# Moving one weight load of a linear-attention and feed-forward kernel from the head of the load queue to a later place

## The chip, the cores and the metric

The kernel runs on one core of a Trainium2 chip. A core has five engines with instruction streams of their own: TensorE (PE, matrix products; its weight loads are listed apart as PEld), VectorE (DVE), ScalarE (ACT), GpSimd (POOL) and SyncE (SP), which here mostly issues transfers. Transfers between the chip's main memory and the on-chip memory, and within the latter, run on 16 DMA engines. The metric is the device time of one execution in microseconds; the median of several executions counts.

## The reference

Two blocks follow each other. The first is a gated linear recurrence for each of 4 batches and 8 heads, over 768 steps with head size 48:

```python
f = 1.0 / (1.0 + np.exp(-f_logit))
for t in range(S):
    state = f[:, :, t, :, None] * state + np.einsum('bhd,bhe->bhde', k[:, :, t], v[:, :, t])
    y[:, :, t] = np.einsum('bhd,bhde->bhe', q[:, :, t], state)
```

The second takes y, with the heads side by side, as x (3072 tokens of 384 values) and computes `(x @ w_a * (x @ w_b)) @ w_out`, with w_a and w_b of 384 x 1536 and w_out of 1536 x 384. The weights arrive as 64-bit floats, everything else as 32-bit floats.

## The kernel before

**Units.** The recurrence is cut into units. A unit is one batch, one half of the sequence (384 steps) and four heads; units 0 and 1 are the two groups of four heads of the first half of batch 0, units 2 and 3 the second half, and so on, 16 in all. For a unit the kernel computes running products of f and of their inverses (`front_parts`: sigmoids on ScalarE, an affine step on GpSimd, scans L333 and L346 on VectorE), multiplies k and q with them (L350), and then has only matrix products and a mask: `scores` (L396), `mask` (L409, VectorE), `turn` and `turned` (k transposed: L421 on PE, copied on ScalarE L430), `gains` (L445), `carried` (sums of states, L474, VectorE), `within` (L504, needs the mask), `across` (L530). `out_of_bank` (L553) copies the result out of PSUM, and `stores_of` (L575) writes it by transfers into `xT`, the input of the feed-forward block; these are the y transfers. Those of units 0 and 1 are issued by SP, by GpSimd and (unit 1) by ScalarE.

**Weights.** `weight_pieces` cuts the weights into pieces in the order of use: pieces 0 and 1 are the first 128 columns of w_b and w_a (384 KB each as 64-bit words), pieces 2 and 3 the next 256 columns of w_b and of w_a (768 KB each), and so on. `load_weights` (L269) issues the load of the next piece on SP into one of four places of `raws4`, or, for pieces 4 and 5, into `groups`. `from_double` makes 32-bit floats of a piece: on ScalarE Abs (L71), Identity (L72) and, later, Sign (L75); on GpSimd a clamp (L73) behind the Abs; on VectorE a shift (L78) and an addition into `w_ba` (L83). `begin(n)` emits the first and second part up to piece n-1, `end(n)` the VectorE part, and `end` also issues the next load from piece 6 on. So piece 3 is read by `begin(4)` and finished by `end(4)`.

**Order.** Each engine carries out its instructions in the order in which they are written. The first part of the program is written out by hand (L1030 to about L1145), until unit 3 is done; `up(0, i)` (L619) are the first products of the feed-forward block, each of six matrix products with columns 128 i to 128 i + 127 of w_b and w_a, and `product` multiplies the two results (copy L640 on ScalarE, L645 on VectorE). After that the remaining units and the feed-forward block are interleaved by a planner that works from stated durations; it comes after all that the change touches.

Around the change the loads stand in this order on SP's queue: f of units 0 and 1; for each of these k, q, a weight piece, v; f of unit 2; pieces 2 and 3; k and q of unit 2. Then SP has nothing to issue until the y transfers of units 0 and 1. After these come f of unit 3 (which waits until GpSimd has filled its buffer, L231), piece 4, v of unit 2, piece 5, k and q of unit 3, piece 6, v of unit 3, piece 7, f of unit 4.

The part of the program behind the change, in the order written: `begin(3)`, `end(2)`, the inverse scans of unit 2, the loads just named, `up(0, 0)`, k and q of unit 2 multiplied, `begin(4)`, sigmoids of unit 3, `end(3)`, `end(4)`, `turn(2)`, `scores(2)`, `up(0, 1)`, `mask(2)`, `product`, `hand_on`, `turned(2)`, `begin(5)`, `within(2)`, `gains(2)`, `up(0, 2)`, `end(5)`, and so on. `up(0, 1)` is the first that needs pieces 2 and 3. The calls `keep_up` (L1020) put matrix products without use between others.

Of the kernel before, what the change touches and what calls it, by code (L numbers as in the profile page):

```python
# [109 lines left out]
def kernel(  # L110
# [29 lines left out]
    with ExitStack() as pools:  # L140
        again, ending = by_quotients(pools, tc, q, k, f_logit, v, moe_w_a, moe_w_b, moe_w_out, out, ident, weights, bad, banks)
# [12 lines left out]
def by_quotients(ctx, tc, q, k, f_logit, v, moe_w_a, moe_w_b, moe_w_out, out, ident, weights, bad, ps_f):  # L154
# [61 lines left out]
    def load_unit(u, names="fkqv"):  # L216
        for do in loads_of(u, names):
            do()

    def loads_of(u, names="fkqv"):  # L220
        if u >= NU:
            return
        b, half, qd = unit(u)
        t = sets[u % NSET]
        cols = slice(half * BLK, half * BLK + BLK)

        def load(to, src):
            nc.sync.dma_start(out=to, in_=src)

        if u - NSET in FIRST and "f" in names:  # L230
            nc.gpsimd.memset(t["f"], 30.0)  # L231
        for nm, src in (("f", f_logit), ("k", k), ("q", q)):
            if nm not in names:
                continue
            if nm == "f" and u in FIRST:

                for par in range(2):
                    row = ((b * H + 4 * qd + par) * D) * S + half * BLK
                    rows = bass.AP(src.tensor, src.offset + row, [[S, R], [2 * D * S, 2], [1, BLK]])
                    yield partial(load, t[nm][R * par:R * par + R], rows)  # L240
                continue
            heads = src[b].rearrange("(n two) d s -> two d n s", two=2)
            for par in range(2):
                yield partial(load, t[nm][R * par:R * par + D], heads[par][:, 2 * qd:2 * qd + 2, cols])
        if "v" in names:
            yield partial(
                load,
                t["v"].rearrange("s n c x -> s n (c x)"),
                v[b, 2 * qd:2 * qd + 2, :, half * NC:half * NC + NC].rearrange("n s c two d -> s n (c two d)"),
            )  # L250
# [5 lines left out]
    def load_weights(n=1):  # L256
        for _ in range(n):
            if len(raws) == len(todo):
                return
            dst, src, (k, m) = todo[len(raws)]  # L260
            raw = dst
            if src.dtype != FP32:

                if len(raws) in EARLY:
                    raw = groups[:, EARLY.index(len(raws))].bitcast(mybir.dt.uint64)
                else:
                    raw = next(raw_places)
                raw = raw[:, 0:k * m].rearrange("p (k m) -> p k m", k=k)
            nc.sync.dma_start(out=raw, in_=src)  # L269
            raws.append(raw)  # L270
# [728 lines left out]
    with tc.manual_schedule():  # L999
# [38 lines left out]
            load_weights()  # L1038
            load_unit(u, "v")
        load_unit(2, "f")  # L1040
        load_weights(2)
        load_unit(2, "k")
        load_unit(2, "q")
        for part in parts[0][1:]:
# [39 lines left out]
        emit_all(parts[2][2])  # L1084


        load_unit(3, "f")
        load_weights()
        load_unit(2, "v")
# [598 lines left out]
```

## Time and profile before

| What | Value |
|---|---|
| Median of 3 runs | 589.61 us (589.22 to 590.11) |
| Profiled execution, time | 590.78 us |
| Profiled execution, span from first to last instruction | 588.9 us |
| PE busy | 568.4 us, 97% of the span |
| VectorE busy | 412.0 us, 70% |
| ScalarE busy | 257.5 us, 44% |
| GpSimd busy | 90.4 us, 15% |
| Mean granted TensorE clock | 0.996 |
| Moved by DMA | 49.42 MB, mean 84 GB/s |
| Loads of w_a in pieces of 768 KB | 4, median 11.8 us from issue to landing |

The profile is of one execution. Times in it count from the start of the span. "L71" is line 71 of the kernel; a line can be that of a helper. A row of the timeline gives start, length (from the first to the last of the instructions merged), engine, line, operation, output and inputs with their sizes, and in brackets how long the engine had been idle and what ended that. SPq stands for transfers issued by SP. A row of the chain gives start, length and what the end of the program waited for in that stretch; "issue" is time in which the engine waited for nothing that the profile shows. DMA share is the mean busy share of the 16 engines; values a little over 1 occur because packets overlap.

### The profile page before, as it was taken

To read this page: it belongs to the slowest core of one execution; us is meant where nothing else is said; L and a number is where in the kernel's file an instruction comes from. 1 tells how busy PE (TensorE), PEld (TensorE's weight loads), DVE (VectorE), ACT (ScalarE), POOL (GpSimd) and SP (SyncE) were. 2 spreads that over 40 slices of the span, in tenths; PEclk is the share of its full clock that TensorE was granted. 3 is DMA by queue.
4 is the path that set the end of the run, shared out by engine and by line. 5 is a ranking of instruction groups with operands and counts; after the bars stand their busy time and mean duration, and the time that the engine had idled before them with its cause. 6 is when DMAs were issued, how large, how long until landed. Compare 5 with 4: busy or idle time off the path is not lost.

```text
span 588.9 us, 13930 instructions
## 1 busy us (share of the span) xinstructions
PE 568.4 (97%) x5796; PEld 510.7 (87%) x5796; DVE 412.0 (70%) x782; ACT 257.5 (44%) x494; POOL 90.4 (15%) x73
## 2 busy tenths in 40 slices
PE   2789999999999999999999999999999999999997
PEld 1546655558999999999999999999999999999997
DVE  6799644599878869876997777837785165836651
ACT  5587668652122554246520444326431345235400
POOL 7365456454000000000000000000000000000000
PEclk9999999999999999999999999999999999999999
DMA  8789489089444123034105400041001100000001
GB/s 198 200 237 303 133 241 297 20 151 186 102 133 107 52 53 102 1 90 100 43 2 129 119 11 2 2 113 36 3 1 48 48 2 0 2 28 0 1 29 32
DMA packets 33576, 49.42 MB, mean 84 GB/s; under 512 B 3984, under 2 KB 25280, under 8 KB 33504
## 3 DMA queue, kind: packets, MB, share of 16 engines
q1 hardware_dynamic: 30000, 42.19, 26.2%
q0 software_dynamic: 3088, 5.92, 5.9%
q8 instruction: 47, 0.77, 0.6%
q10 hardware_dynamic: 416, 0.34, 0.2%
q14 instruction: 25, 0.20, 0.1%
HBM read 33.23 MB, written 4.72 MB: 64 GB/s over the span
## 4 chain that ended last, share of the span: by engine, by line
PE 91%; DVE 5%; issue 2%; ACT 1%; DMA 1%; SPq 0%; DVEq 0%; ACTq 0%
PE ps_f L745 39%; PE ps_f L847 28%; PE ps_f L619 15%; PE ps_y L504 2%; PE ps_y L530 2%; PE ps_x L445 1%; PE ps_x L396 1%; PE ps_x L421 1%; DVE inv L346 1%; DVE q_in L350 1%; DVE groups L333 1%; DMA f_in<-in_f_logit_dram 1%; DVE at L409 0%; DVE groups L737 0%; DVE spare L346 0%
## 5 line engine op out<-in xcount | busy, mean ns | idle before, releaser
L619 PE MATMUL ps_f<-xT,w_ba 128*128 128x384 f32 x288 | 95.8, 490 | 0.7 <-DVE w_ba L83 0.6
L1335 ACT COPY sums<-ps_f 128x384 f32<-128x384 f32 x120 | 57.6, 480 | 76.2 <-PE ps_f L745 68.5
L619 PEld LDWEIGHTS ps_f<-xT,w_ba 128*128 128x128 f32 x288 | 53.7, 190 | 37.8 <-ACT spare L75 1.2
L1335 ACT COPY groups<-ps_f 128x384 f32<-128x384 f32 x120 | 57.6, 481 | 61.3 <-PE ps_f L745 40.7
L745 PE MATMUL ps_f<-xT,w_ba 128*128 128x192 f32 x384 | 78.5, 327 | 0.0
L745 PEld LDWEIGHTS ps_f<-xT,w_ba 128*128 128x128 f32 x384 | 64.7, 190 | 0.3
L73 POOL TENSOR_SCALAR sums<-sums 128x768 f32<-128x768 f32 (+1 forms) x20 | 52.6, 2629 | 34.5 <-ACT sums L71 34.4
L745 PE MATMUL ps_f<-groups,w_ba 128*128 128x192 f32 x288 | 54.9, 326 | 0.0
L745 PE MATMUL ps_f<-x_sums,raw 128*128 128x192 f32 x288 | 53.7, 330 | 0.5 <-DVE groups L737 0.5
L329 POOL TENSOR_SCALAR inv<-inv 128x768 f32<-128x768 f32 x14 | 13.6, 972 | 261.2 <-ACT inv L326 217.0
L847 PE MATMUL ps_f<-w_out,sums 128*128 128x192 f32 x288 | 51.9, 327 | 0.0
L847 PE MATMUL ps_f<-w_out,groups 128*128 128x192 f32 x288 | 51.8, 329 | 0.0
L847 PE MATMUL ps_f<-spare,sums 128*128 128x192 f32 x288 | 49.5, 327 | 0.0
L745 PEld LDWEIGHTS ps_f<-x_sums,raw 128*128 128x128 f32 x288 | 47.0, 190 | 2.6 <-ACT sums L1335 1.0
L745 PEld LDWEIGHTS ps_f<-groups,w_ba 128*128 128x128 f32 x288 | 48.0, 190 | 0.1
L847 PEld LDWEIGHTS ps_f<-w_out,groups 128*128 128x128 f32 x288 | 47.2, 190 | 0.7
L847 PEld LDWEIGHTS ps_f<-w_out,sums 128*128 128x128 f32 x288 | 47.3, 190 | 0.2
L847 PEld LDWEIGHTS ps_f<-spare,sums 128*128 128x128 f32 x288 | 47.0, 190 | 0.1
L737 DVE TENSOR_TENSOR sums<-ps_f,sums 128x384 f32<-128x384 f32 x60 | 32.7, 553 | 16.9 <-PE ps_f L745 12.9
L737 DVE TENSOR_TENSOR sums<-sums,groups 128x768 f32<-128x768 f32 x36 | 34.3, 953 | 11.8 <-ACT groups L1335 11.2
L745 PE MATMUL ps_f<-xT,raw 128*128 128x192 f32 x192 | 39.4, 328 | 0.2 <-ACT groups L1335 0.2
L745 PE MATMUL ps_f<-x_sums,w_ba 128*128 128x192 f32 x192 | 39.3, 327 | 0.0
(150 smaller groups left out, 850.7 us busy)
## 6 DMA issues: line engine op xcount, KB each, us to landing
raw<-w_ba POOLq DMA_DIRECT2D x11, 512.0 KB, 8.3
k_in<-in_k_dram SPq DMA_DIRECT2D x32, 144.0 KB, 4.4
q_in<-in_q_dram SPq DMA_DIRECT2D x32, 144.0 KB, 4.5
v_in<-in_v_dram SPq DMA_DIRECT2D x16, 288.0 KB, 5.1
raw<-in_moe_w_out_dram SPq DMA_DIRECT2D x6, 768.0 KB, 4.8
out_dram<-o SPq DMA_DIRECT2D x22, 192.0 KB, 1.9
f_in<-in_f_logit_dram SPq DMA_DIRECT2D x28, 144.0 KB, 3.0
xT<-y SPq DMA_DIRECT2D x44, 72.0 KB, 2.1
```

The lines of the kernel that those rows point to most:

```text
L73: nc.gpsimd.tensor_scalar(h, h, HI_MIN, HI_MAX, ALU.max, ALU.min)
L329: nc.gpsimd.tensor_scalar(inv, inv, EXP_K, 1.0, ALU.mult, ALU.add)
L333: nc.vector.tensor_tensor_scan(F[:, c], F[:, c], none, math.exp(MIDDLE), ALU.mult, ALU.add)
L346: nc.vector.tensor_tensor_scan(inv[:, w], inv[:, w], none[:, 0:C], first, ALU.mult, ALU.add)
L350: nc.vector.tensor_tensor(halves(t[nm]), halves(t[nm]), by, ALU.mult)
L504: nc.tensor.matmul(ps[p][e:e + D, o:o + SUB], lhsT=t["v"][r, n, c, h * D:h * D + D], rhs=at[r, h, o:o + SUB], start=o == 0, stop=True, ski ...
L530: nc.tensor.matmul(ps[p][e:e + D, o:o + SUB], lhsT=st[j][r, n], rhs=qf[r, tokens(n, c, p)], start=False, stop=True, skip_group_check=True,)
L619: nc.tensor.matmul(ps[nm][:, 0:BLK], lhsT=w[:, kt, ft * 128:ft * 128 + 128], rhs=xT[blk][:, kt], start=kt == 0, stop=kt == NKT - 1,)
L737: nc.vector.tensor_tensor(to, x, y, op)
L745: nc.tensor.matmul(ps[:, g], lhsT=sums_of_w[name][:, g, 128 * j:128 * j + 128], rhs=sums_of_x[blk][name], start=start and g == 0, stop=Tru ...
L847: nc.tensor.matmul(to, lhsT=x[:, i // 2, i % 2], rhs=w[:, NI * (i % 2) + i // 2], start=start and i == 0, stop=i == HFT - 1, skip_group_ch ...
L1335: do(*args)
```

## The change

The fourth weight piece (piece 3) is no longer loaded together with piece 2, ahead of k and q of unit 2. Its load is issued on SP behind the y transfers of units 0 and 1, ahead of f of unit 3. The order of all other loads, the places they go to and all computation stay as they are.

```diff
@@ -1038,7 +1038,7 @@
             load_weights()
             load_unit(u, "v")
         load_unit(2, "f")
-        load_weights(2)
+        load_weights()
         load_unit(2, "k")
         load_unit(2, "q")
         for part in parts[0][1:]:
@@ -1084,6 +1084,7 @@
         emit_all(parts[2][2])
 
 
+        load_weights()
         load_unit(3, "f")
         load_weights()
         load_unit(2, "v")
```

## The prediction

> **What bounds the kernel now.** First the page: PE is busy 568.4 of 588.9 us, so 20.5 us of PE idleness is all there is to win or to add to. The chain that ended last shows where it lies. From 40.34 us it is PE almost without a break, so what delays or advances PE there goes to the end nearly whole; before that it is mostly VectorE. The chain around the change (start, length, what):
>
> ```profile
> 24.41 0.84 PE ps_x L530 x34
> 25.24 2.27 issue
> 27.52 0.32 PE ps_x L530 x4
> ...
> 28.20 1.88 PE ps_f L530 x40
> 30.10 0.55 DVE groups L553
> ...
> 39.86 0.44 DVE w_ba L83
> 40.34 4.22 PE ps_f L619 x12
> ```
>
> PE stands for 2.27 us inside `across(0)`, waiting for nothing shown; VectorE waits for the `across(1)` behind it and starts at 30.10. I read the stall as a late page of PE's instructions: a shorter one (0.35 us, until 22.69) lies exactly 128 matmul-and-weight-load pairs earlier, 256 instructions. The page counts the fetches of queue q8:
>
> ```profile
> q8 instruction: 47, 0.77, 0.6%
> ```
>
> 47 fetches of 16 KB. Asked in tenths of a microsecond, they begin at 20.0, 24.6 and 28.6 us and last 1.10, 1.49 and 1.13 us (share x 16 engines x 0.1 us).
>
> Then the timeline of what the moved piece (number 3: w_a, columns 128 to 383) feeds:
>
> ```profile
> 31.31 1.16 SPq L575 DMA_DIRECT2D xT<-groups  x2
> 33.11 0.80 SPq L228 DMA_DIRECT2D f_in<-in_f_logit_dram  x2
> 33.23 0.87 ACT L71 ACTIVATE sums<-raw 128x768 f32<-128x768 f32 x1
> 34.19 2.80 POOL L73 TENSOR_SCALAR sums<-sums 128x768 f32<-128x768 f32 x1 [1.11 <-ACT sums L71]
> 40.87 0.55 DVE L78 TENSOR_SCALAR sums<-sums 128x768 uint32<-128x768 uint32 x1
> 41.56 1.72 DVE L83 CUSTOM_DVE_ANT_0 w_ba<-sums,spare 128x512 uint16<-128x512 uint16 x3
> 43.00 0.94 PEld L619 LDWEIGHTS ps_f<-xT,w_ba 128*128 128x128 f32 x4 [0.43 <-DVE w_ba L83]
> 43.21 0.95 DVE L409 TENSOR_TENSOR at<-ps_x,causal 128x768 f32<-128x768 f32 x1
> ```
>
> The last two y stores of SP end at 32.47. ScalarE reads piece 3 at 33.23 (`begin(4)`), GpSimd clamps it until 36.99, VectorE finishes it at 40.87 (`end(4)`), then makes `mask(2)`, for which `within(2)` waits on PE. So piece 3 now has 3.9 us of slack between GpSimd and VectorE, but it feeds the chain.
>
> Last, the DMA questions. The windows show the engines saturated (share 1.0 or more) from 4 to 24 us, nearly idle from 25 to 30, saturated again from 36.5 to 55. Time to landing of single loads of 768 KB: piece 3, the piece of 33.95 us, the one of 59.07:
>
> ```profile
> raw<-in_moe_w_a_dram SPq DMA_DIRECT2D x1, 768.0 KB, 12.5
> ...
> groups<-in_moe_w_b_dram SPq DMA_DIRECT2D x1, 768.0 KB, 5.3
> ...
> raw<-in_moe_w_a_dram SPq DMA_DIRECT2D x1, 768.0 KB, 4.2
> ```
>
> The clock matters too (us, busy times, granted clock, DMA share, GB/s):
>
> ```profile
> 25.00:28.20 3.20, 0.93 (x22) 0.68 (x14) 1.54 (x4) 0.33 (x1) 0.71 (x1) 1.00 0.05 13
> 28.30:31.60 3.30, 3.30 (x43) 2.55 (x40) 1.44 (x4) 1.94 (x5) 1.28 (x2) 0.50 0.23 65
> ```
>
> After the stall PE ran 3.4 us at half clock, and `across(1)` lies in it.
>
> **What the Trainium skill says.** "Runtime: NRT & Kernel Launch", section Instruction fetch mechanics: instructions come in 16 KiB blocks of 256 by the sequencer's own DMA queue, a cost "mostly hidden". Block size and spacing agree; hidden it is not here (2.27 us). "DMA: Bandwidth & Descriptors", section Queues, rings and completion order: each DMA engine takes queues in turn, a packet at a time, and its own ring in order. So a fetch can wait behind loads. The trace agrees: fetch 24.6 came 1.9 us after PE crossed its page at 22.69 with the engines busy, fetch 28.6 1.1 us after the crossing at 27.52 with them idle. "TensorE: Matmul & The Clock Gate", Part 1: half clock after an idle window of about 3.4 us, and the windows run free. The 3.4 us at 0.50 agree, and the phase may differ between executions.
>
> **The change part by part.**
>
> *Taken from the front.* One issue of 0.39 us on SP at 13.45: k and q of unit 2 are issued somewhat earlier. They land at 26.3 to 27.3 (14.25 + 12.0 to 16.9 + 10.4) and are first multiplied at 36.80: worth nothing, 9 us of cover. What counts is 768 KB less in the engines. The drain at 24.4 moves up by 2 to 4 us (at 390 to 200 GB/s, both seen), so around the crossing at 22.69 they are idle or nearly. A fetch then costs as the third did: 1.1 to start, 1.13 to move, and from its end to PE's resumption 1.43 (26.09 to 27.52): 3.7 us, so PE resumes at 26.4 instead of 27.52: gain 1.1. Bounds: 0, if the fetch was not late because of these loads; 1.45 if the stall at 22.34 goes as well. I take 0.9, since k and q still keep some engines busy at 22.7.
>
> *The clock.* A shorter stall leaves its 3.4 us window busier. At full clock 40 matmuls of `across(1)` take 0.74 us (48 take 0.89 at 49.90) instead of 1.90: up to 1.15 more for VectorE. It doesn't reach the end, as the next part shows.
>
> *Put in behind the y stores.* One SP issue, 0.39 us, at 32.47; the f load behind it is held until a GpSimd memset ends at 33.08 anyway, so the issue hides in a gap of 0.64 (without it, 0.4 late for f, which is wanted only at 36.44). SP's stores run one after another from y(0)'s copies, so their end moves with the stall alone: 32.47 - 0.9 = 31.57. Landing: 4.2 to 5.3 us by the rows above; y packets still run for the first 0.7 us, so I take 4.8: 36.4. Then ScalarE Abs to GpSimd's start 0.96, clamp 2.80, hand-overs 0.06: VectorE can finish the piece from 40.2, against 40.87 before. Without the wait for the piece VectorE would be there at 39.97, or near 38.8 at full clock. So the late piece takes the rest of the gain: **-0.65 us** on the path to `mask(2)` and PE. Zero is at a landing at 37.05.
>
> *What queues behind the waiting ScalarE.* `begin(4)` moves from 33.23 to 36.4, and the next seven pieces of ScalarE work with it. From its start to piece 4's Abs took 7.4 us (33.23 to 40.60): now 43.6. Sigmoids of unit 3: 39.6, wanted by the scan at 43.9. `kT`: 43.2 to 43.9, wanted by `gains(2)` behind `within(2)`, at 44.5. Piece 4: clamp done at 47.5, wanted at 47.7. Piece 5: clamp done near 51, VectorE was there at 50.52; PE needs the second half of those weights at about 51.9. ScalarE's gap before 50.88 (3.98 us) absorbs the lag. Margins of 0.2 to 1, all positive: cost 0, and the gain goes if they are 1 us worse.
>
> *DMA behind it.* 768 KB more from 31.6 on push later landings by some 2 us, less the gap at 33.5: piece 4 from 39.25 to about 41.5 (wanted 43.6), v of unit 2 from 40.1 to 42 (wanted 43.8), piece 5 from 43.3 to 45.8 (wanted 46.9). Some SP issues follow landings (unit 3's v at 39.28, right after piece 4's at 39.25); these move too, to data wanted after 50.
>
> Sum: 588.9 - 0.65 = 588.25 span; with the 1.88 around it (590.78 profiled) 590.1. The median, 589.61, is 1.17 below the profiled execution; from it, 589.61 - 0.65 = **589.0 us**.
>
> **Rivals.**
> *The whole stall goes (faster).* Both page waits vanish (1.45) and the piece lands as the undisturbed one did: 32.47 - 1.45 + 4.2 = 35.2, finished from 39.05: -1.8, 587.8. For: the third fetch, quick in idle engines. Against: y packets share the engines.
> *The landing becomes the wait (slower).* The stall stays and the piece shares the engines with y, f and piece 4: 6.0 us, between 5.3 and the 7.6 of the piece before it at 12.68. 32.47 + 6.0 = 38.5, finished from 42.3: +1.4, 591.0. It decides from a landing at 38.2 (+1.2). For: all SP loads lag once the engines are full. Against: only y stands ahead of it.
> *The timed executions already run `across(1)` at full clock.* Then VectorE was at `end(4)` at about 39.8 before, and 40.2 afterwards is +0.3: 589.9. For: profiled is 1.17 above the median, about the 1.15 of the cold clock. Against: profiling may cost that by itself.
>
> **How the numbers follow.** Likeliest 0.42 (landing 35.6 to 37.0: 588.2 to 589.6); whole stall gone 0.24; landing late 0.20; clock already full 0.14. 0.2% is 1.18 us, about what a measurement of this kernel can tell from no change. Faster: the second case and a quarter of the first, 0.34; slower: the third, 0.20; same: the rest, 0.46. The range runs from the whole stall's end, 587.7, to most of the late landing, 590.8.
>
> **What would show it.** Right: the issue gap in `across(0)` down to 1.0 to 1.6 us; no half clock after it; ScalarE idle some 4 us until the Abs of piece 3, near 36.4; `end(4)` straight after the clamp; PE going on with `within(2)` near 43.8 instead of 44.49. Wrong: a gap still of 2.3 us, so loads do not delay pages; piece 3 landing beyond 38; or PE waiting at 47 to 53 us for pieces 4 and 5, because ScalarE's lag is not absorbed.

## The result and the profile after

The changed kernel takes 594.04 us (median of 9 runs, 592.53 to 595.69); the kernel before, run beside it, 590.25 us. The ratio is 1.0049, 95% interval 1.0032 to 1.0067 (ratios in this document are the record's comparison of all runs of both kernels, not quotients of two medians). It is slower, by an interval that leaves out 1; the prediction was 589.0 us with a range up to 590.8. The profiled execution of the changed kernel took 594.04 us with a span of 592.2 us, 3.3 more than before.

The chain that ended last, in the changed kernel, around the change (start, length, what):

```profile
25.25 0.28 issue
25.54 0.32 PE ps_x L530 x4
...
30.54 5.27 DMA raw<-in_moe_w_a_dram
...
35.83 0.93 ACT sums L71
...
36.85 2.88 POOL sums L73
...
39.76 0.57 DVE sums L78
...
40.45 0.83 DVE w_ba L83
...
41.33 4.21 PE ps_f L619 x6
45.54 1.46 PE ps_x L504 x48
```

The stall of 2.27 us in `across(0)` is 0.28 us here, and PE is through it 2 us sooner (25.54 instead of 27.52). All the same the moved load is now a link of the chain: load, Abs, clamp, shift, addition, and then the w_a half of `up(0, 1)`. The profile lists each of the six products of `up(0, 1)` as two matmul records. In the kernel before all twelve records stood in the chain as one piece of 4.22 us; here six of them, those with w_a, take 4.21 us alone.

The timeline of the changed kernel between 36 and 49 us (start, length, engine, line, operation, output and inputs, in brackets the idle time before and what ended it):

```profile
36.47 2.20 PE L619 MATMUL ps_f<-xT,w_ba 128*128 128x384 f32 x6
41.33 4.21 PE L619 MATMUL ps_f<-xT,w_ba 128*128 128x384 f32 x6 [2.65 <-DVE w_ba L83]
41.87 0.94 DVE L409 TENSOR_TENSOR at<-ps_x,causal 128x768 f32<-128x768 f32 x1
45.47 1.53 PE L504 MATMUL ps_x<-at,v_in 64*48 64x64 f32 x48
```

and of the kernel before, where both halves of `up(0, 1)` are one row:

```profile
40.34 4.22 PE L619 MATMUL ps_f<-xT,w_ba 128*128 128x384 f32 x12
44.49 0.89 PE L504 MATMUL ps_x<-at,v_in 64*48 64x64 f32 x48
```

PE does the w_b half of `up(0, 1)` early, at 36.47, and then stands for 2.65 us between the two halves, until piece 3 is finished. The mask that `within(2)` waits for is begun at 41.87, earlier than before (43.21), but `within(2)` itself comes later (45.47 instead of 44.49), because the w_a half stands ahead of it on PE and takes twice its time. The windows say why (of the changed kernel; us, busy times and instructions of PE, PEld, DVE, ACT, POOL, granted clock, DMA share, GB/s):

```profile
36.90:40.40 3.50, 1.77 (x6) 0.76 (x4) 0.75 (x2) 3.44 (x5) 3.42 (x2) 1.00 1.07 383
40.40:44.00 3.60, 2.67 (x4) 1.51 (x5) 3.55 (x6) 3.54 (x11) 1.52 (x3) 0.55 1.08 263
44.00:47.60 3.60, 3.60 (x89) 2.47 (x89) 1.74 (x3) 3.57 (x5) 3.28 (x2) 0.51 1.05 333
47.60:51.00 3.40, 3.40 (x22) 2.11 (x17) 2.77 (x8) 1.40 (x2) 2.20 (x1) 1.00 1.07 307
```

After the stretch in which PE was busy for half of the time, it ran at half clock for some 7 us (granted clock 0.55 and 0.51 in the two rows behind it). In the kernel before the clock was full there:

```profile
40.30:44.60 4.30, 4.26 (x19) 2.23 (x22) 4.16 (x9) 4.27 (x6) 2.99 (x1) 1.00 1.10 232
44.60:48.60 4.00, 4.00 (x97) 2.89 (x98) 3.83 (x10) 2.26 (x3) 3.20 (x2) 1.00 1.05 363
```

Where the two traces come apart (starts in us):

| Step on PE | before | after | difference |
|---|---|---|---|
| `across(0)` goes on | 27.52 | 25.54 | -1.98 |
| w_b half of `up(0, 1)` | 40.34 | 36.47 | -3.87 |
| w_a half of `up(0, 1)` | about 42.4 | 41.33 | -1.1 |
| `within(2)` | 44.49 | 45.47 | +0.98 |
| `up(0, 2)` | 45.83 | 47.76 | +1.93 |
| `across(2)` | 49.90 | 51.83 | +1.93 |
| `across(3)` | 69.57 | 71.50 | +1.93 |
| last twelve matmul records | 583.45 | 585.49 | +2.04 |

(42.4 is 40.34 and half of the 4.22 us that both halves took.) So the whole difference is made between 41 and 48 us: 2.1 us because the w_a half takes 4.2 instead of 2.1, 0.95 because `within(2)` and `gains(2)` take 2.29 instead of 1.34, less the 1.1 us that the w_a half began sooner. The rest of the span's 3.3 us lies behind the last product, a stretch of 3.4 us before and 4.6 after; over the traces of this study it is 3.3 to 5.4 us, in no order with what was changed.

### The profile page after: what moved, and what is told of

It reads as the page before. It is cut to its first block, busy times and chain, and to the rows that moved or that the text cites. A ratio compares the mean times of both kernels' runs of the same rounds, so it can differ in the third digit from the quotient of the medians.

```text
span 592.2 us, 13930 instructions
## 1 busy us (share of the span) xinstructions
PE 569.0 (96%) x5796; PEld 510.6 (86%) x5796; DVE 411.4 (69%) x782; ACT 257.5 (43%) x494; POOL 90.0 (15%) x73
## 4 chain that ended last, share of the span: by engine, by line
PE 90%; DVE 4%; DMA 1%; issue 1%; ACT 1%; SPq 1%; POOL 0%; DVEq 0%; ACTq 0%
PE ps_f L745 39%; PE ps_f L847 28%; PE ps_f L619 15%; PE ps_y L504 2%; PE ps_y L530 2%; PE ps_x L445 1%; PE ps_x L396 1%; PE ps_x L421 1%; DMA raw<-in_moe_w_a_dram 1%; DVE q_in L350 1%; DVE groups L333 1%; DVE inv L346 1%; DMA f_in<-in_f_logit_dram 1%; POOL sums L73 0%; DVE at L409 0%
## 5 line engine op out<-in xcount | busy, mean ns | idle before, releaser
L619 PE MATMUL ps_f<-xT,w_ba 128*128 128x384 f32 x288 | 98.0, 498 | 4.4 <-DVE w_ba L83 2.7
L737 DVE TENSOR_TENSOR sums<-ps_f,sums 128x384 f32<-128x384 f32 x60 | 32.7, 553 | 16.8 <-PE ps_f L745 12.9
```

The costliest lines, as they stand in the source:

```text
L619: nc.tensor.matmul(ps[nm][:, 0:BLK], lhsT=w[:, kt, ft * 128:ft * 128 + 128], rhs=xT[blk][:, kt], start=kt == 0, stop=kt == NKT - 1,)
L737: nc.vector.tensor_tensor(to, x, y, op)
```

## The experiments

**Theory.** PE needs piece 3 for the w_a half of `up(0, 1)` and stands idle for it; that wait and the half clock that follows it are the loss. The rivals: the traffic of the load in its new place delays other transfers; the place matters and not the lateness; the page stall in front decides.

**The changed kernel once more.** No edit.

> The changed kernel unaltered, beside the others on one chip. Expected: ratio to the kernel before 1.005. In its trace, counted from the moment PE resumes in across of unit 0: the load is issued 5.0 us later and lands 5.2 later still, the VectorE part of piece 3 starts 14.2 us after the resumption, and PE stands idle ahead of the w_a half of the second up product. If the idle time trips the clock, within of unit 2 starts 19.9 us after the resumption, if not 17.5 to 18.5; in the kernel before and in the experiment behind the queries it was 16.2 to 17.0.

Measured: 593.63 us, ratio 1.0033, 1.0017 to 1.0049 (expected 1.005). Its chain:

```profile
25.72 1.53 issue
...
32.24 5.30 DMA raw<-in_moe_w_a_dram
...
43.03 3.67 PE ps_f L619 x6
46.71 0.82 PE ps_x L504 x48
```

The page stall is back, 1.53 us after one of 1.26, with the load no longer in front: PE goes on in `across(0)` at 27.25 us, not at 25.54. The wait between the halves is 2.65 us again, to the hundredth. Both things that meet there hang on the same event, PE's going on in `across(0)`: the load was issued 5.0 us after it in both traces (behind the y stores, which copy what `across` computes), and the w_b half ended 13.1 us after it in both. A faster front moves the load and PE together and leaves the wait as it is. `within(2)` began 19.4 us after that event, between the 19.9 expected with half clock and the 18.5 at most without it: the half clock was there, for 3.4 us instead of some 7.

**Front alone.** The kernel before, without any load of piece 3; its conversion reads the words of piece 2.

```diff
-            nc.sync.dma_start(out=raw, in_=src)
+            if len(raws) != 3:
+                nc.sync.dma_start(out=raw, in_=src)
...
-    nc, dst, raws[i], shape[0], ...
+    nc, dst, raws[2 if i == 3 else i], shape[0], ...
```

> The kernel before without any load of piece 3; its conversion reads the words of piece 2, so nothing is late and nothing is added behind 31 us. The output is not the reference's (these columns of w_a get the words of w_b). It has the front of the changed kernel alone. Theory now (the front's gain was mostly the luck of one execution): PE's two page gaps before 28 us add up to between 0.3 and 2.5 us, and the ratio to the kernel before is 0.998 to 1.000. Rival (the prediction's step: 768 KB less in front is worth 1 to 2 us): ratio 0.9965 or less.

Measured: 591.10 us, ratio 0.9999, 0.9986 to 1.0012. In its trace the two stalls are 1.2 and 1.5 us. Taking 768 KB from the front gains nothing. Over the traces with all of piece 3 loaded in front by SP (before, and two experiments below) `across(0)` goes on at 27.52, 26.06 and 25.95 us; with nothing of it in front (the two of the changed kernel, and four experiments) at 25.54, 27.25, 27.33, 27.23, 26.55 and 27.98. The means are 26.5 and 27.0. (Half of the piece in front gave 26.87, the load issued by ScalarE 27.95; the kernel with shifted pages has no stall there.)

This trace and that of the changed kernel's second run have nearly the same front (27.33 and 27.25), so they can be laid side by side. (In the latter the filler products behind the front ran at half clock, from 29.0 to 32.4 us; `up(0, 0)` begins at 32.21 and at 32.13 us all the same.) Timeline of PE, first of this experiment, where `up` is L620 and `within` L505:

```profile
39.41 4.14 PE L620 MATMUL ps_f<-xT,w_ba 128*128 128x384 f32 x12 [0.73 <-DVE w_ba L83]
43.48 0.89 PE L505 MATMUL ps_x<-at,v_in 64*48 64x64 f32 x48
```

and of the changed kernel:

```profile
38.18 2.20 PE L619 MATMUL ps_f<-xT,w_ba 128*128 128x384 f32 x6
43.03 3.67 PE L619 MATMUL ps_f<-xT,w_ba 128*128 128x384 f32 x6 [2.65 <-DVE w_ba L83]
46.64 0.89 PE L504 MATMUL ps_x<-at,v_in 64*48 64x64 f32 x48
```

`within(2)` comes 3.16 us later: the w_a half begins at 43.03 instead of 41.5 (39.41 and half of 4.14), which is 1.5 us, and takes 3.67 instead of 2.07 (half of 4.14), which is 1.6: the half clock. `across(3)` follows at 71.72 instead of 68.56, again 3.16.

**Late traffic alone.** The kernel before, with the same 768 KB loaded a second time at the new place, into a place that is free by then.

```diff
+        nc.sync.dma_start(out=raws4[:, 0:PIECE].rearrange("p (k m) -> p k m", k=NKT), in_=todo[3][1])
         load_unit(3, "f")
```

> The kernel before with everything it has, plus a second load of piece 3's words at the place where the change puts the load, into a free buffer that nobody reads. It has the added traffic of the changed kernel alone. Theory (traffic alone costs little): the f of unit 3 lands some 2 us later and ScalarE waits for it, the ratio to the kernel before is 1.000 to 1.001. Rival (traffic is what costs): ratio 1.003 or more.

Measured: 590.77 us, ratio 0.9992, 0.9972 to 1.0011. The traffic was there and delayed what came behind it, by the timeline of this kernel:

```profile
37.61 0.94 ACT L326 ACTIVATE spare<-f_in,less 128x768 f32<-128x768 f32 x1 [3.64 <-DMA f_in<-in_f_logit_dram]
```

ScalarE stood 3.64 us for f of unit 3, and no loss shows in the time. As a cause of a loss of 0.3 to 0.5% the traffic falls.

**No wait.** The changed kernel, whose conversion of piece 3 reads the words of piece 2; the late load is issued, and nothing waits for it.

```diff
-    nc, dst, raws[i], shape[0], ...
+    nc, dst, raws[2 if i == 3 else i], shape[0], ...
```

> The changed kernel, but the conversion of piece 3 reads the words of piece 2, long there, so nothing waits for the late load; the load itself stays where the change put it. The output is not the reference's, since these columns of w_a get the words of w_b. Theory (the loss is the wait for the piece and the clock after it, not the traffic behind it): the gap in across of unit 0 stays at 0.3 us, PE runs through the second up product from about 36.5 to 40.7 us at full clock, and the time is 3 to 4 us under the kernel before (ratio about 0.994). Rival (the added traffic after 31 us delays pieces 4 and 5 and what follows): the gain is lost again by 53 us and the ratio is 0.998 or more.

Measured: 591.74 us, ratio 1.0015, 1.0003 to 1.0027. In its timeline the halves are one again, at full clock:

```profile
38.00 4.47 PE L619 MATMUL ps_f<-xT,w_ba 128*128 128x384 f32 x12
```

Most of the loss is gone with the wait. The gain that the expectation hoped for (0.994) is not there; its number is the one that was named for the rival. That forecast rested on a stall of 0.3 us in front, and here the two stalls were 0.57 and 1.12 us; the front alone shows no gain and the late traffic alone, just above, no cost, so the number speaks against the gain and not for the traffic. Of what is left, 0.15%, the lower end is close to nothing, and the two experiments that hold its parts (front alone, late traffic alone) show nothing; whether it is real stays open.

**Half as late.** The changed kernel, with piece 3 in two loads of 384 KB: its second 128 columns in front of unit 2's keys, its first at the new place.

```diff
+    def load_part(cols):
+        dst, src, (k, m) = todo[3]
+        if len(raws) == 3:
+            raws.append(next(raw_places)[:, 0:k * m].rearrange("p (k m) -> p k m", k=k))
+        nc.sync.dma_start(out=raws[3][:, :, cols], in_=src[:, :, cols])
...
         load_weights()
+        load_part(slice(128, 256))
         load_unit(2, "k")
...
-        load_weights()
+        load_part(slice(0, 128))
         load_unit(3, "f")
```

> The changed kernel with its third piece in two halves of 128 columns (384 KB each): the second half is loaded in front of unit 2's keys, the first half at the new place behind the y stores. Theory (PE stands idle between the two halves of up(0,1) because the words of piece 3 land too late, and that idle time costs the clock as well): the late half is only 384 KB, which lands about 3.3 us after its issue (63.40 and 66.66 us in the trace of before) instead of 5.3, some 8.7 us after PE resumes in across(0); VectorE ends the conversion about 1.6 us earlier than in the changed kernel, PE's wait for w_ba between the halves falls from 2.65 us to between 0.4 and 1.1, and the ratio is between 0.999 and 1.002. Rival (the new place itself, behind the y stores and ahead of f and piece 4, is what costs, whatever the size of the load): the ratio stays at 1.003 to 1.005.

Measured: 591.79 us, ratio 1.0008, 0.9989 to 1.0028. The half load took 4.12 us to land, not 3.3, so VectorE's shift stood at 13.1 us after PE's going on in `across(0)` (40.01 after 26.87) instead of 14.2 as in the changed kernel: 1.1 us sooner, not 1.6. The timeline:

```profile
41.58 2.20 PE L626 MATMUL ps_f<-xT,w_ba 128*128 128x384 f32 x6 [1.02 <-DVE w_ba L83]
```

The wait is 1.02 us, and the w_a half behind it ran at full clock (2.20 us). The place is that of the changed kernel, the order too; the lateness is less, and so is the loss. That speaks against the rival of the place.

**Later still.** The changed kernel, with the load of piece 3 behind f of unit 3 and piece 4. `place_of_third` only sets the piece's place in `raws` aside.

```diff
+    def place_of_third():
...
-        load_weights()
+        place_of_third()
         load_unit(3, "f")
         load_weights()
+        nc.sync.dma_start(out=raws[3], in_=todo[3][1])
```

> The changed kernel with the load of the third piece another two places later: f of unit 3 and piece 4 go ahead of it. Theory (PE waits in up(0,1) for exactly this load): it lands 3 to 4 us later than in the changed kernel, PE's wait between the halves of up(0,1) grows from 2.65 us to about 6, with two or more windows at half clock, and the ratio is 1.007 to 1.012. Rival (the lateness of piece 3 isn't what the end of the kernel depends on, and the clock alone makes the difference by chance): the ratio stays at 1.003 to 1.005.

Measured: 596.85 us, ratio 1.0085, 1.0053 to 1.0117. By the timeline:

```profile
46.27 4.05 PE L624 MATMUL ps_f<-xT,w_ba 128*128 128x384 f32 x6 [5.11 <-DVE w_ba L83]
```

The load landed at 40.88, 12.9 us after PE's going on in `across(0)` (27.98) instead of 10.3, so 2.6 later; the wait grew by 2.46 to 5.11 us, and the clock was at half from 43.2 to 50.0. The size of the step was overestimated (3 to 4 us later, a wait of 6), the ratio was within what the theory expected.

The series in one place. The third column is the time from PE's going on in `across(0)` to the start of `within(2)`, which leaves out the stalls in front:

| Kernel | Wait between the halves, us | To `within(2)`, us | Ratio |
|---|---|---|---|
| front alone | 0 | 16.15 | 0.9999 |
| no wait | 0 | 15.85 | 1.0015 |
| half as late | 1.02 | 16.84 | 1.0008 |
| changed | 2.65 and 2.65 | 19.93 and 19.39 | 1.0049 and 1.0033 |
| later still | 5.11 | 22.27 | 1.0085 |

**PE kept busy.** The changed kernel, with three products without use (six matmul records) between the two halves.

```diff
+                if (blk, ft, nm) == (0, 1, "a"):
+                    keep_up(3, ps[nm])
```

> The changed kernel, with three matrix products without use put between the w_b half and the w_a half of the second up product (about 2.1 us of PE work where PE now stands idle for 2.65 us); everything else as in the changed kernel. Theory (the idle time trips the clock): no half clock between 40 and 48 us, the w_a half of that product takes 2.1 instead of 4.2 us, and the next two stages 0.8 and 0.7 instead of 1.5 and 1.05; about 3 us less than the changed kernel, so 1 us less than the kernel before (ratio to before 0.998). Rival (the late loads of pieces 4 and 5 or ScalarE's lag set the pace): PE then waits at the next stages instead, and the time stays within 0.5 us of the changed kernel (ratio 1.005).

Measured: 592.47 us, ratio 1.0030, 1.0019 to 1.0041. The timeline:

```profile
39.66 2.20 PE L621 MATMUL ps_f<-xT,w_ba 128*128 128x384 f32 x6
41.70 2.10 PE L1022 MATMUL ps_f<-groups,ident 128*128 128x384 f32 x6
43.63 2.10 PE L621 MATMUL ps_f<-xT,w_ba 128*128 128x384 f32 x6
```

The gap is filled, and there was no half clock after 40 us: the w_a half took 2.10 us. The filling ran 0.6 us beyond the moment at which the weights were ready (about 43.0), which takes part of the gain back; in this trace the clock had been at half from 29.5 to 36.3 us as well, behind the page stalls, and that brought the w_b half late. From PE's going on in `across(0)` (27.23) to `within(2)` (45.66) it was 18.43 us, 1.0 to 1.5 less than in the changed kernel: in the trace most of the half clock's cost is gone, and what the wait costs in time is left. The gain in time is small (the mean is 1.5 us over its kernel before, that of the changed kernel's second set 2.5 over its own), the intervals overlap, and the 0.998 that was expected was missed. That the wait costs time is shown by the runs; the clock's share of it is read from traces.

**Other places in front.** The kernel before, with piece 3 behind k and q of unit 2, still ahead of the y stores:

```diff
-        load_weights(2)
+        load_weights()
         load_unit(2, "k")
         load_unit(2, "q")
+        load_weights()
```

> The kernel before, with the load of piece 3 behind the third unit's keys and queries instead of ahead of them; still at the front. Theory (what frees PE's page is the smaller load of the DMA engines before 25 us): the engines stay full as before, the gap in across of unit 0 stays above 1.5 us, the piece lands near 27 us and is there when ScalarE wants it, and the time is that of the kernel before within 0.5 us. Rival (the place relative to keys and queries matters): the gap falls to 0.3 us as in the changed kernel, and the time is 2 us or more under the kernel before.

Measured: 591.18 us, ratio 1.0005, 0.9991 to 1.0019; the page stalls were 0.2 and 1.0 us in its trace, where the expectation had the second above 1.5; the time is as expected. And the kernel before, with piece 3 issued by ScalarE (`load_weights` has the queue as an argument there); its trace has the issue at 21.81 us, not near 23.8:

```diff
-        load_weights(2)
+        load_weights()
...
+        load_weights(queue=nc.scalar)
```

> The kernel before, with the load of piece 3 issued by ScalarE behind the first part of piece 2's conversion, near 23.8 us, when the DMA engines have just drained, instead of at 13.45 us by SyncE. Theory: the gap in across of unit 0 shrinks to about 0.3 us as in the changed kernel, the piece lands near 28.5 us, before ScalarE wants it at about 30.7, and PE runs through without the idle time and without the half clock; 3 to 4 us under the kernel before (ratio about 0.994). Rival (the gap and the clock in the front do not matter for the end): ratio 1.000 within 0.001.

Measured: 593.28 us, ratio 1.0045, 1.0028 to 1.0061: slower where it was to be faster. In its trace PE crossed into the new page at 23.12, the fetch began at 25.5, 2.4 us later, and the stall was the longest of all, 2.63 us, with half clock from 28.4 to 35.2. The moved load kept the DMA engines at about 400 GB/s up to 25.5 us, just when that fetch began. That a load issued so close to the crossing holds up the fetch fits this one trace; that this is what makes the kernel slower is not shown by an experiment.

**Pages shifted.** The kernel before, with the 8 matmul records of a `keep_up` replaced by 114 of small products:

```diff
-        keep_up(4, ps_f[idle[-1]])
+        small(57, ps_f[idle[-1]])
```

> The kernel before with four filler products of 384 columns (8 matmul records) replaced by 57 small ones (114 records of about the same time together), so that PE's instruction stream is 212 instructions longer there and its 256-instruction page ends fall 106 matmul records earlier in the work that follows. Theory (the gaps are page ends): the gaps after the 4th record of gains of unit 1 and after the 34th of across of unit 0 vanish; if any remain they are 26 records further in the work (inside gains of unit 1, behind the wait for the mask, and in across of unit 1) and shorter, and the time is 1 to 2 us under the kernel before (ratio 0.997 to 0.998). Rival (the gaps are something else, tied to these places): they stay where they were and the ratio is 1.000.

Measured: 594.30 us, ratio 1.0042, 1.0024 to 1.0061. The time says little, because the small products took 7.26 us where I had counted on about as long as the 2.85 us that they replaced, and the clock fell to half while they ran (from 21.0 to 27.8 us). But the stalls moved: `across(0)` is unbroken, and the waits of PE have instead (us in all, times, longest)

```profile
PE ps_x L530 <- issue: 0.5, 1, 0.5
```

in `across(2)`, behind its 47th matmul record. The places can be counted in the traces, with all that PE's sequencer carries out: weight loads, matmul records and the few instructions between them. In the kernel before 449 instructions stand ahead of the short stall (220 matmul records, 221 weight loads and 8 others, mostly semaphore instructions) and 705 ahead of the long one, behind the 36th record of `across(0)`; here 1473 stand ahead of the stall (729, 729 and 15). 705 is 449 and 256, and 1473 is 705 and three times 256. The Trainium skill, "Runtime: NRT & Kernel Launch", section Instruction fetch mechanics, has the blocks of 256 instructions; these traces agree. The two boundaries between 705 and 1473 show no stall, so not each crossing costs one. That the stalls are pages is thus shown; that the load in front makes them longer in sum is not borne out (front alone, above).

## Why the prediction was wrong

The step that decides is the sum in "Put in behind the y stores": it set the landing of piece 3 against VectorE in the trace of before and found 0.65 us to gain, where the date that counts is PE's, at the w_a half of `up(0, 1)`. PE waited there for 2.65 us, and the half clock behind the wait stood at nothing in the sum. The gain that was booked in front failed as well.

**"Taken from the front" failed.** It took the 2.27 us of one execution for the rule and the load for its cause, and booked 0.9 us. The ratio of the front alone is 0.9999. The price of one page, 3.7 us from entering it to going on in the next, was right: 3.73 in the trace of the front alone (23.60 to 27.33), in the changed kernel's second (23.52 to 27.25) and in that with PE kept busy, against 4.83 in the kernel before (22.69 to 27.52). But the 4.83 is not the rule with the piece in front, where two more traces have 3.73 and 3.45; and the entry, which the step held at 22.69, moved. With all of the piece in front the first stall was 0.16 to 0.35 us in three traces; with nothing of it there it was 0.57 to 1.56 in five of six and missing in one, that of the result. So in the three traces named the entry came 0.8 to 0.9 us later, which takes most of the 1.1 us back. Why the first stall grows stays open. The sign named for the step appeared by luck, and misled: the gap in the changed kernel's first trace was 0.28 us, and the kernel was slower.

**"The clock" was right for the stretch it spoke of and stopped there.** `across(1)` ran at full clock in the changed kernel's trace (its 40 records took 1.15 us instead of 1.90; the step had 0.74), and VectorE began the mask 1.34 us sooner. The same rule was not applied to the new wait: there the half clock costs 1.6 us in the pair with equal fronts, 3 us in the pair of the result. Over all runs only a rough size can be had: one minus the granted clock, times the span, has a mean of 2.7 us in the changed kernel's second set of runs and 1.6 in the kernel before beside it. So of the 2.5 us by which the means of these runs differ about 1.1 may be clock and 1.4 the later start. It is an estimate, since half clock that costs the end nothing counts in it too: under the filler products in front, and behind the last product (0.4 us of it in the trace of before, 0.9 in that of the result).

**"Put in behind the y stores" was right in its parts and wrong in its sum.** The landing took 5.27 and 5.30 us (taken: 4.8, bounds 4.2 to 5.3) and fell at 35.8 and 37.5 us (36.4); from landing to VectorE's shift it was 3.9 us in both (3.8). VectorE did take the piece at 39.76 in the result's trace, sooner than 40.87 (41.46 in the second). But the sum compared this with the 40.87 of one execution, in which VectorE was late behind an `across(1)` at half clock, and not with PE. In the written order PE has only the w_b half to do before it needs piece 3. That half waits for `end(3)`, which a faster VectorE does sooner; so what made the front faster also brought PE sooner to the wait. The mark was not a landing at 37.05 but about 33.2 us in the result's trace: 35.81 less the 2.65 of waiting.

**"What queues behind the waiting ScalarE" and "DMA behind it" held.** In the changed kernel PE waits for no later weights, and late traffic alone gives 0.9992. Piece 4 took 6.9 us to land instead of 5.3, piece 5 10.2 instead of 8.3, about the 2 us booked.

**The rival "the landing becomes the wait"** had the place and the sign, with a chance of 0.20, and a size too small: +1.4 us against 2 to 3 by the two ratios. Its condition, a landing beyond 38.2 us, was met in neither trace of the changed kernel (35.8 and 37.5); it had the same wrong mark, and no clock. **The rival of the full clock** was right that the timed executions of the kernel before differ in it: of the 75 beside the first experiments those with a granted clock of 0.998 or more have a mean of 590.4, the others of 591.8 us. Whether the clock or the stall ahead of it makes these 1.4 us is not shown. The three runs of 589.61 us, from which the forecast counted, are at the lower edge; the later sets of 9 to 75 runs have medians of 590.25 to 591.3. That is 0.6 us of the miss in the result's own set, up to 1.7 in the others, and no part of the ratio.

## What to carry to other kernels

When a load is put off, compare its landing with the first instruction that any in-order engine can't pass without it, and work out when that engine arrives there in the new schedule, not in the old one: both often hang on the same event, and then speeding up what is ahead doesn't shrink the wait. A wait of TensorE has to be priced with the clock that it may cost: here a wait of 2.65 us made PE's next step 1.5 us later and cost 1.6 us more in half clock (the pair with equal fronts), and one of 1.02 us cost no clock. A stall of which the length changes from execution to execution should be read from several traces before a gain is booked on it.

## What the hardware showed that was not expected

The Trainium skill, "TensorE: Matmul & The Clock Gate", section HAM oscillation, gives as the rule "no PE-idle gaps >~3.4µs". Here a gap of 2.65 us was followed by half clock in both traces of the changed kernel, once for about 7 us and once for 3.4; the measurement decides. The clock fell before the gap was over, 2.1 and 2.2 us into it (40.7 and 42.6 us); in the 3.4 us before that PE had been busy for 1.38 and 1.18 us. In the first case the clock stayed low through a window in which PE was at work for 2.67 of 3.60 us. The length of the gap alone doesn't decide: a page stall of 1.12 us in one trace (no wait) and of 1.53 in two (changed again, PE kept busy) was followed by half clock, one of 1.53 us in another (front alone) was not. What decides there is not shown.

The kernel before, unchanged, spreads over 588.3 to 595.1 us in the two larger sets of runs. The page stalls (0.2 to 2.3 us in the three traces with piece 3 loaded by SP in front and the pages unshifted) and the half clock that may follow them are the part of this that the traces show.
